# Moving bias and decoding work between engines in a fused attention and mixing kernel

## Chip, cores and metric

The kernel runs on one core of a Trainium2 chip. The metric is device time in microseconds, the median of several runs; lower is better. Engines: PE (TensorE: matmuls and transposes), DVE (VectorE), ACT (ScalarE), POOL (GpSimd), SP (issues the DMAs here). Each engine works through its own queue in order.

## What is computed

Two batches of 768 tokens, 8 heads of 64. Attention with a local window, a few global keys and a linear distance bias, then a two-layer channel mixer behind a layer norm, then a rotation by learned angles with token mixing.

```python
scores = q @ k.T / sqrt(64) + bias        # bias = -slope[h] * dist, heads h = 0..7
keep   = (key < n_global) | ((rel >= 0) & (rel < n_local))
attn   = softmax(where(keep, scores, -1e9)) @ v
x = attn + relu(layer_norm(attn) @ w_ch1) @ w_ch2
theta = x @ w_theta;  zr, zi = x * cos(theta), x * sin(theta)
u = x + w_tok_r @ zr + w_tok_i @ zi
out = u + relu(u @ w_ch)
```

The weights arrive as 64-bit floats ("pieces" of 128x512) and are turned into 32-bit floats on the chip.

## The kernel before

**Blocks and pairs.** The 12 blocks of 128 queries are worked in the order 0, 6, 1, 2, 3, 4, 5, 7, ... 11 (`SEQ`; a name such as e1_2_0 is batch 1, block 2 of that batch, head pair 0). Blocks 0 and 6 are first in their batches and see 128 keys, the others 256. Four head pairs make a block. `attention` is a pipeline over the 48 pairs: at step n it emits the scores of pair n (`scores`), the transposes of the probabilities of pair n-2 (`flip_probs`), and the values of pair n-3 (`values`). After a block come its copy from PSUM and scaling (`finish_x`: ACT writes xs, PE transposes it into xp, DVE scales), the layer norm, and a transposition for the mixer (`make_xt`: xnp on PE, xth on ACT, xtl on DVE).

**A pair** is: two score matmuls on PE; on DVE, per head, one operation that adds the bias and finds the maximum (L204, to nm and e); on ACT, per head, the exponential with its sum (L211); PE transposes e into pt; a copy of pt to pts on DVE for pairs 0 and 3 of a block (L226) and on ACT for pairs 1 and 2 (L224); PE multiplies with the values into xa.

**The bias** of each head is a table of 128 x 384. `make_bias` makes the part for first blocks on DVE before any score; the part for later blocks ("old", 128x256, eight heads) comes after the fourth head's maximum, on ACT (L148).

**Weight pieces.** `load_to` issues DMAs of raw pieces into three buffers. `decode` turns a raw piece into f32: for pieces 0 to 15 one activation (L314) and three DVE operations (L322 to L324); for later ones two activations (L314, L318) and two DVE operations (L319, L320). `split_w` then divides a piece into a high part (ACT, L340) and a low part (POOL or DVE, L341). Pieces 2f and 2f+1 belong to MLP group f. During attention, groups 0 to 3 (pieces 0 to 7) are used: for every chunk of two blocks, MLP steps `mlp_h` (12 matmuls, L369) and `mlp_o` (6 matmuls, L392). Pieces 8 to 15 wait in eight buffers for the next round.

**The order** of each engine's queue is set by the scheduler of the framework from the order of emission and priorities; `tc.issue_after(ins)` keeps an instruction behind another one (`behind_maximum(n)` uses it with the n-th maximum). `steps_to(n)` emits attention steps up to n, and the calls between them put the first decodings in the emission order.

Of the kernel before, what the change touches and what calls it, by code (L numbers as in the profile page):

```python
# [32 lines left out]
def kernel(ctx, tc, q, kwin, v, n_pair, g_ln, wall, out):  # L33
# [77 lines left out]
    nc.vector.memset(zero, 0.0)  # L111
    bias = [at.tile([P, WIN + P], BF16, name=f"bias{h}") for h in range(H)]

    maxima = []

    def behind_maximum(n):
        return tc.issue_after(maxima[n]) if n is not None else ExitStack()
# [1 line left out]
    def make_bias():  # L119

        n = WIN + P
        rel, key, a = (at.tile([P, n], F32, tag="xn", name=f"bias_{x}", bufs=3) for x in ("rel", "key", "a"))
        io = dict(allow_small_or_imprecise_dtypes=True)
        v_ = nc.vector
        own = rel[:, P:n].rearrange("p (t c) -> p t c", c=P)
        old, first = slice(0, WIN), slice(WIN, n)
        nc.gpsimd.iota(own, [[0, 2], [-1, P]], base=0, channel_multiplier=1, **io)
        nc.gpsimd.iota(key[:, first], [[1, P]], base=0, channel_multiplier=0, **io)
        nc.gpsimd.iota(rel[:, 0:PREV], [[-1, PREV]], base=PREV, channel_multiplier=1, **io)
        nc.gpsimd.iota(key[:, PREV:P], [[1, GLOB]], base=0, channel_multiplier=0, **io)  # L130
        v_.memset(rel[:, PREV:P], FAR)
        v_.memset(key[:, 0:PREV], FAR)
        v_.memset(key[:, P:WIN], FAR)
        v_.tensor_scalar(a[:, P:n], rel[:, P:n], 0.0, FAR, ALU.is_lt, ALU.mult)
        v_.tensor_tensor(rel[:, P:n], rel[:, P:n], a[:, P:n], ALU.max)
        yield
        load_n()
        for part in (first, old):
            r, k_, a_ = rel[:, part], key[:, part], a[:, part]
            with behind_maximum(3 if part is old else None):  # L140
                v_.tensor_scalar(a_, r, nl, NEG, ALU.is_ge, ALU.mult)
                v_.tensor_scalar(k_, k_, ng, NEG, ALU.is_ge, ALU.mult)
            v_.tensor_tensor(r, a_, r, ALU.subtract)
            v_.scalar_tensor_tensor(r, k_, nl, r, ALU.subtract, ALU.max)
            for h in range(H):
                slope = 2.0 ** (-8.0 * (h + 1) / H)
                if part is old:
                    nc.scalar.activation(bias[h][:, part], r, AF.Copy, scale=slope / SCALE)  # L148
                else:
                    v_.tensor_scalar(bias[h][:, part], r, slope / SCALE, None, ALU.mult)  # L150
            yield

    def slot(name):
# [30 lines left out]
    def scores(b, i, p, startup):  # L184
        nk = WIN if i else P
        b0 = 0 if i else WIN
        if p == 0:
            stat[b, i] = (
                at.tile([P, H], F32, tag="nm", name=f"nm{b}_{i}", bufs=2),
                at.tile([P, H], F32, tag="sm", name=f"sm{b}_{i}", bufs=2),  # L190
            )
        nm, sm = stat[b, i]
        qb, kb = qt[b, i], kt[b, i]
        s = [ps("h" if startup and p % 2 else "s", [P, nk], f"s{b}_{i}_{p}_{j}") for j in range(2)]
        k0 = WIN - nk
        for j in range(2):
            rows = slice(j * D, (j + 1) * D)
            nc.tensor.matmul(s[j], qb[rows, p, :], kb[rows, p, k0:WIN], start=True, stop=True)  # L198
        if startup:
            spin("o", f"spin{b}_{p}", 2)  # L200
        e = at.tile([P, 2, nk], F32, tag="p", name=f"e{b}_{i}_{p}", bufs=3)
        for j in range(2):
            h = 2 * p + j
            r = nc.vector.tensor_tensor_reduce(  # L204
                out=e[:, j, :], in0=s[j], in1=bias[h][:, b0:b0 + nk], scale=-SCALE, scalar=3.0e38,
                op0=ALU.add, op1=ALU.min, accum_out=nm[:, h:h + 1],
            )
            maxima.append(r.ins)
        for j in range(2):
            h = 2 * p + j  # L210
            nc.scalar.activation(e[:, j, :], e[:, j, :], AF.Exp, bias=nm[:, h:h + 1], scale=-1.0, accum_out=sm[:, h:h + 1])  # L211
        e_t[b, i, p] = e

    def flip_probs(b, i, p, startup):
# [5 lines left out]
            for c in range(nb):  # L220
                nc.tensor.transpose(pt[:, j, c, :], e[:, j, c * P:(c + 1) * P], ident)
        pts = at.tile([P, 2, nb, P], F32, tag="pt", name=f"pts{b}_{i}_{p}", bufs=2)
        if p % 3:
            nc.scalar.activation(pts, pt, AF.Copy)  # L224
        else:
            nc.vector.tensor_copy(pts, pt)  # L226
# [71 lines left out]
    def load_to(n):  # L298
        while n_staged[0] <= min(n, len(order) - 1):
# [3 lines left out]
            stage[i] = r  # L303
            n_staged[0] += 1

    def decode(i, out):

        n = n_decoded[0]
# [2 lines left out]
        assert order[n] == i  # L311
        r = stage.pop(i)
        load_to(n + NRAW)
        nc.scalar.activation(out, r.bitcast(F32)[:, :, 1], AF.Copy, scale=2.0**-112)  # L314
        t = rawp.tile([P, DM], I32, tag="dec", name=f"dec{i}", bufs=1)
        o = out.bitcast(I32)
        if i >= 4 * GROUP:
            nc.scalar.activation(t, r.bitcast(U32)[:, :, 0], AF.Copy, scale=2.0**-29 * (1 - 2.0**-15), bias=-0.4999)  # L318
            nc.vector.scalar_tensor_tensor(t, o, 3, t, ALU.logical_shift_left, ALU.bitwise_or)  # L319
            nc.vector.scalar_tensor_tensor(o, r[:, :, 1], -2**31, t, ALU.bitwise_and, ALU.bitwise_or)  # L320
# [277 lines left out]


    def general():  # L600
        es = ExitStack()
        ga = es.enter_context(tc.tile_pool(name="ga", bufs=1))
        row = ga.tile([P, S], F32, name="g_row")
# [175 lines left out]
    def steps_to(n):  # L779
        while n_step[0] < n:  # L780
            next(st, None)
            n_step[0] += 1
# [6 lines left out]
    next(bias_steps)  # L789
    load_to(1)  # L790
    nc.sync.dma_start(gbc, g_ln.partition_broadcast(P))
    steps_to(4)
    split_w(0)
    steps_to(done_at(0))
    split_w(1)
# [126 lines left out]
```

## Time and profile before

| | us |
|---|---|
| median of 3 runs | 571.13 (570.25 to 571.83) |
| profiled execution, its own time | 572.38 |
| its span | 570.5 |
| PE busy | 555.1 |
| DVE busy | 365.7 |
| ACT busy | 282.7 |
| POOL busy | 121.9 |

The span is what the profiler recorded between first and last instruction; the execution's own time lies a little over it. A busy time is the union of an engine's instructions. In lines of the timeline and of the chain, the first number is the start within the span, the second the duration.

### The profile page before, as it was taken

The numbers are of one execution on the slowest core, as the hardware profiler recorded it, in microseconds if no ns is written. First come the engines' busy times: TensorE is split into PE (matmuls) and PEld (weight loads), VectorE is DVE, ScalarE is ACT, GpSimd is POOL, SyncE is SP. The second block draws the span as 40 slices with busy tenths as digits, with TensorE's granted clock in tenths as the row PEclk, the third lists the DMA queues.
The fourth block names the chain that finished last, engine by engine and source line by source line (L and its number), as shares of the span: only waits on it lengthen the run. The fifth ranks groups of instructions, "written<-read, shape, count | busy, mean of one in ns | idle before, by whom it ended". The sixth has DMA issues, their size and how long they took to land.

```text
span 570.5 us, 9281 instructions
## 1 busy us (share of the span) xinstructions
PE 555.1 (97%) x3531; PEld 461.4 (81%) x3532; DVE 365.7 (64%) x789; ACT 282.7 (50%) x647; POOL 121.9 (21%) x103
## 2 busy tenths in 40 slices
PE   8898999999999999999999999999999999999996
PEld 4465676777888899999989888889888888888885
DVE  6899988857458732278784524462699879871442
ACT  5886864636226511166663415561578777740110
POOL 1455420000002100030300202231033347730000
PEclk9999999999999999999999999999999999999999
DMA  8965655500003410026552000000243200000112
GB/s 262 317 214 187 215 192 204 167 1 2 0 1 109 150 37 1 1 80 198 167 185 74 1 1 1 2 1 0 79 144 132 91 1 1 1 1 1 74 68 86
DMA packets 18548, 49.18 MB, mean 86 GB/s; under 512 B 2240, under 2 KB 4288, under 8 KB 18496
## 3 DMA queue, kind: packets, MB, share of 16 engines
q1 hardware_dynamic: 18496, 48.51, 25.7%
q8 instruction: 30, 0.49, 0.4%
q14 instruction: 22, 0.18, 0.1%
HBM read 45.35 MB, written 3.15 MB: 85 GB/s over the span
## 4 chain that ended last, share of the span: by engine, by line
PE 64%; ACT 1%; DVE 1%; issue 0%; DVEq 0%; ACTq 0%
PE acc L545 17%; PE op L392 17%; PE hp L369 17%; PE thm L480 6%; PE ch L591 6%; PE xp L284 1%; ACT wt L314 0%; ACT xth L285 0%; DVE hl L374 0%; DVE w2l L341 0%; DVE x2all L381 0%; ACT w L314 0%; ACT k L488 0%; ACT k L487 0%; ACT s L493 0%
## 5 line engine op out<-in xcount | busy, mean ns | idle before, releaser
L369 PE MATMUL hp<-xth,w1h 128*128 128x256 f32 x384 | 109.0, 284 | 0.0
L369 PE MATMUL hp<-xth,w1l 128*128 128x256 f32 x384 | 108.7, 283 | 0.0
L369 PE MATMUL hp<-xtl,w1h 128*128 128x256 f32 x384 | 108.4, 282 | 0.0
L374 DVE SCALAR_TENSOR_TENSOR hl<-hp,hh 128x256 fp32r<-128x256 f32 x96 | 40.3, 420 | 79.9 <-ACT hh L373 79.7
L373 ACT ACTIVATE hh<-hp 128x256 fp32r<-128x256 f32 x96 | 36.1, 377 | 95.5 <-PE hp L369 95.5
L545 PE MATMUL acc<-tokh,z 128*128 128x512 f32 (+1 forms) x320 | 79.6, 337 | 0.0
L392 PE MATMUL op<-w2h,hh 128*128 128x512 f32 x192 | 76.9, 401 | 0.7 <-ACT hh L373 0.5
L369 PEld LDWEIGHTS hp<-xth,w1h 128*128 128x128 f32 x384 | 72.6, 189 | 6.1 <-issue 1.5
L369 PEld LDWEIGHTS hp<-xtl,w1h 128*128 128x128 f32 x384 | 72.5, 189 | 5.9 <-issue 1.7
L392 PE MATMUL op<-w2h,hl 128*128 128x512 f32 x192 | 76.1, 396 | 0.0
L392 PE MATMUL op<-w2l,hh 128*128 128x512 f32 x192 | 76.1, 396 | 0.0
L369 PEld LDWEIGHTS hp<-xth,w1l 128*128 128x128 f32 x384 | 72.6, 189 | 1.7 <-issue 1.5
L545 PEld LDWEIGHTS acc<-tokh,z 128*128 128x128 f32 x320 | 55.3, 189 | 7.2
L211 ACT ACTIVATE e<-e,nm 128x256 f32<-128x256 f32 (+1 forms) x96 | 46.2, 482 | 25.3 <-DVE nm L204 23.8
L545 PE MATMUL acc<-tokl,z 128*128 128x512 f32 (+1 forms) x160 | 54.0, 338 | 0.0
L341 POOL TENSOR_TENSOR w1l<-w,w1h 128x512 fp32r<-128x512 f32 x16 | 22.3, 1393 | 136.9 <-ACT w1h L340 136.9
L381 DVE SCALAR_TENSOR_TENSOR x2all<-op,rsall,x2all 128x512 f32<-128x512 f32 x60 | 42.8, 743 | 6.8 <-PE op L392 6.8
L507 POOL TENSOR_TENSOR x2all<-xth,xtl 128x512 f32<-128x512 f32 x12 | 18.3, 1528 | 121.2 <-DVE k L499 116.2
L392 PEld LDWEIGHTS op<-w2h,hl 128*128 128x128 f32 x192 | 36.1, 188 | 9.2 <-DVE hl L374 0.4
L204 DVE CUSTOM_DVE_ANT_0 e<-s,bias 128x256 f32<-128x256 f32 (+1 forms) x96 | 35.5, 393 | 11.6 <-PE s L198 10.9
L457 DVE TENSOR_TENSOR tokl<-wt,tokh 128x512 fp32r<-128x512 f32 x36 | 33.9, 951 | 11.3 <-ACT tokh L456 11.1
L392 PEld LDWEIGHTS op<-w2h,hh 128*128 128x128 f32 x192 | 36.4, 190 | 5.6 <-ACT hh L373 0.7
(155 smaller groups left out, 1072.4 us busy)
## 6 DMA issues: line engine op xcount, KB each, us to landing
raw<-in_wall SPq DMA_DIRECT2D x58, 512.0 KB, 3.3
k<-in_kwin SPq DMA_DIRECT2D x10, 512.0 KB, 5.6
q<-in_q SPq DMA_DIRECT2D x12, 256.0 KB, 4.3
vc<-in_v SPq DMA_DIRECT2D x12, 256.0 KB, 3.3
out<-o SPq DMA_DIRECT2D x8, 256.0 KB, 2.0
vw<-in_v SPq DMA_DIRECT2D x10, 192.0 KB, 2.6
out<-o SPq DMA_DIRECT2D x8, 128.0 KB, 2.0
vw<-in_v SPq DMA_DIRECT2D x10, 64.0 KB, 3.5
```

Of the source, the lines that this page charges most:

```text
L204: r = nc.vector.tensor_tensor_reduce(out=e[:, j, :], in0=s[j], in1=bias[h][:, b0:b0 + nk], scale=-SCALE, scalar=3.0e38, op0=ALU.add, op1=A ...
L211: nc.scalar.activation(e[:, j, :], e[:, j, :], AF.Exp, bias=nm[:, h:h + 1], scale=-1.0, accum_out=sm[:, h:h + 1])
L341: (nc.vector if d and f >= GROUP else nc.gpsimd).tensor_tensor(lo, s, hi.bitcast(F32), ALU.subtract)
L369: nc.tensor.matmul(hp, l, r[:, kk, :], start=(n == 0), stop=(n == 3 * KD - 1))
L373: nc.scalar.activation(hh, hp, AF.Relu)
L374: nc.vector.scalar_tensor_tensor(hl, hp, 0.0, hh.bitcast(F32), ALU.max, ALU.subtract)
L381: nc.vector.scalar_tensor_tensor(x2[t], o, rsall[:, t:t + 1], x2[t], ALU.mult, ALU.add)
L392: nc.tensor.matmul(op_t[c][j], l, r, start=(f == fs[0] and n == 0), stop=(f == fs[-1] and n == 2))
L457: nc.vector.tensor_tensor(lo, src, hi.bitcast(F32), ALU.subtract)
L480: nc.tensor.matmul(mp, l[:, kk, :], r[:, kk, :], start=(n == 0), stop=(n == 3 * KD - 1))
L545: mm = nc.tensor.matmul(o, l[:, dsl], r[:, sl], start=first and not (paired and d % 2), stop=end and not (paired and d % 2 == 0))
L591: nc.tensor.matmul(mp, l[:, kk, es], r, start=(kk == 0 and m == 0), stop=(kk == KD - 1 and m == 2))
```

## The change

It moves work between engines and places in the order:

- The bias for later blocks is written by POOL (eight tensor_scalars of 128x256) instead of ACT.
- The first activations of pieces 0 and 1 are held behind the exponentials of pairs 5 and 6; `split_w(0)` is emitted after seven attention steps instead of four.
- Pieces 8 to 15 are decoded by two activations and two DVE operations instead of one and three, and the first activation of each is held behind the last exponential of a later block: the eighth block in `SEQ` for pieces 8 and 9, the ninth for 10 and 11, the tenth for 12 and 13, the eleventh for 14 and 15.
- From the seventh block in `SEQ` on, all four copies of pt to pts are by ACT.

```diff
-    maxima = []
+    maxima, exps = [], []
...
-                if part is old:
-                    nc.scalar.activation(bias[h][:, part], r, AF.Copy, scale=slope / SCALE)
-                else:
-                    v_.tensor_scalar(bias[h][:, part], r, slope / SCALE, None, ALU.mult)
+                (nc.gpsimd if part is old else v_).tensor_scalar(bias[h][:, part], r, slope / SCALE, None, ALU.mult)
...
-            nc.scalar.activation(e[:, j, :], e[:, j, :], AF.Exp, bias=nm[:, h:h + 1], scale=-1.0, accum_out=sm[:, h:h + 1])
+            r = nc.scalar.activation(e[:, j, :], e[:, j, :], AF.Exp, bias=nm[:, h:h + 1], scale=-1.0, accum_out=sm[:, h:h + 1])
+        exps.append(r.ins)
...
-        if p % 3:
+        if p % 3 or SEQ.index(b * NQ + i) >= 6:
             nc.scalar.activation(pts, pt, AF.Copy)
...
+    def behind_exponentials(i):
+
+        n = 5 + i if i < 2 else NPAIR * (7 + (i - 2 * GROUP) // 2) + 3 if 2 * GROUP <= i < 4 * GROUP else None
+        return tc.issue_after(exps[n]) if n is not None and n < len(exps) else ExitStack()
...
-        nc.scalar.activation(out, r.bitcast(F32)[:, :, 1], AF.Copy, scale=2.0**-112)
+        with behind_exponentials(i):
+            nc.scalar.activation(out, r.bitcast(F32)[:, :, 1], AF.Copy, scale=2.0**-112)
...
-        if i >= 4 * GROUP:
+        if i >= 2 * GROUP:
...
-    steps_to(4)
+    steps_to(7)
     split_w(0)
```

In the orders below the names carry batch, block and pair (w0 is piece 0, raw0 its raw form, dec0 the help buffer of its decoding), and each row is one instruction or several alike. The changed file has its lines 3 lower or 3 to 5 higher: L208 there is L211, L222 is L224, L318 and L322 are L314 and L318, L326 to L328 are L322 to L324.

ACT's queue at the start, before the change, from the second pair's exponentials on:

```order
L211 ACTIVATE e0_0_2_216,sm0_0_167<-e0_0_2_216,nm0_0_166 128x128
L148 ACTIVATE bias0_93<-bias_rel_111 128x256
...
L148 ACTIVATE bias7_100<-bias_rel_111 128x256
L211 ACTIVATE e0_0_2_216,sm0_0_167<-e0_0_2_216,nm0_0_166 128x128
L211 ACTIVATE e0_0_3_233,sm0_0_167<-e0_0_3_233,nm0_0_166 128x128 x2
L224 ACTIVATE pts0_0_1_241<-pt0_0_1_238 128x256
L314 ACTIVATE w0_246<-raw0_204 128x512
L314 ACTIVATE w1_256<-raw1_206 128x512
L211 ACTIVATE e1_0_0_290,sm1_0_282<-e1_0_0_290,nm1_0_281 128x128 x2
L224 ACTIVATE pts0_0_2_298<-pt0_0_2_295 128x256
```

Six more bias copies stand between the two shown; the decodings of pieces 0 and 1 are ahead of the fifth pair's exponentials (e1_0_0). With the change:

```order
L208 ACTIVATE e0_0_2_216,sm0_0_167<-e0_0_2_216,nm0_0_166 128x128
L222 ACTIVATE pts0_0_1_241<-pt0_0_1_238 128x256
L208 ACTIVATE e0_0_3_233,sm0_0_167<-e0_0_3_233,nm0_0_166 128x128 x2
L208 ACTIVATE e1_0_0_264,sm1_0_256<-e1_0_0_264,nm1_0_255 128x128 x2
L222 ACTIVATE pts0_0_2_272<-pt0_0_2_269 128x256
L208 ACTIVATE e1_0_1_283,sm1_0_256<-e1_0_1_283,nm1_0_255 128x128 x2
L208 ACTIVATE e1_0_2_302,sm1_0_256<-e1_0_2_302,nm1_0_255 128x128 x2
L248 ACTIVATE xs0_314<-xa0_0_243 128x512
L318 ACTIVATE w0_324<-raw0_204 128x512
L318 ACTIVATE w1_334<-raw1_206 128x512
L208 ACTIVATE e1_0_3_357,sm1_0_256<-e1_0_3_357,nm1_0_255 128x128 x2
```

The bias copies are gone from ACT, and both decodings stand seven rows later, behind the copy of block 0's result.

DVE's queue where the third block's maxima begin, with the change (before it, decoding 0 and decoding 1 stood ahead of the last pair of the second block, and the scaling of block 0 behind the first maximum here):

```order
L326 TENSOR_SCALAR dec0_330<-w0_324 128x512
L254 TENSOR_TENSOR x2all_66<-xp0_318,sm0_0_167 128x512
L327 SCALAR_TENSOR_TENSOR dec0_330<-w0_324,dec0_330 128x512
L266 BN_STATS bn0_370<-x2all_66 128x6
L328 SCALAR_TENSOR_TENSOR w0_324<-raw0_204,dec0_330 128x512
L267 BN_AGGR mv0_371<-bn0_370 128x2
L201 ISA e0_1_0_394,nm0_1_388<-s0_1_0_0_390,bias0_93 128x256
L201 ISA nm0_1_388 128x1
L326 TENSOR_SCALAR dec1_338<-w1_334 128x512
L274 TENSOR_SCALAR rsall_69<-mv0_371 128x1
L201 ISA e0_1_0_394,nm0_1_388<-s0_1_0_1_391,bias1_94 128x256
```

The first maximum of the third block (e0_1_0) is now behind all of decoding 0 and the statistics of block 0.

ACT's queue in a late run of attention (tenth to eleventh block), before:

```order
L211 ACTIVATE e1_3_3_1615,sm1_3_1433<-e1_3_3_1615,nm1_3_1432 128x256 x2
L224 ACTIVATE pts1_3_1_1625<-pt1_3_1_1620 128x512
L211 ACTIVATE e1_4_0_1646,sm1_4_1641<-e1_4_0_1646,nm1_4_1640 128x256 x2
L224 ACTIVATE pts1_3_2_1656<-pt1_3_2_1651 128x512
L211 ACTIVATE e1_4_1_1675,sm1_4_1641<-e1_4_1_1675,nm1_4_1640 128x256 x2
L211 ACTIVATE e1_4_2_1695,sm1_4_1641<-e1_4_2_1695,nm1_4_1640 128x256 x2
L250 ACTIVATE xs9_1711<-xa1_3_1627 128x512
```

and with the change:

```order
L208 ACTIVATE e1_3_3_1615,sm1_3_1433<-e1_3_3_1615,nm1_3_1432 128x256 x2
L222 ACTIVATE pts1_3_1_1625<-pt1_3_1_1620 128x512
L318 ACTIVATE w12_2266<-raw12_2152 128x512
L208 ACTIVATE e1_4_0_1646,sm1_4_1641<-e1_4_0_1646,nm1_4_1640 128x256 x2
L222 ACTIVATE pts1_3_2_1656<-pt1_3_2_1651 128x512
L318 ACTIVATE w13_2299<-raw13_2193 128x512
L208 ACTIVATE e1_4_1_1675,sm1_4_1641<-e1_4_1_1675,nm1_4_1640 128x256 x2
L222 ACTIVATE pts1_3_3_1685<-pt1_3_3_1680 128x512
L322 ACTIVATE dec13_2303<-raw13_2193 128x512
L208 ACTIVATE e1_4_2_1695,sm1_4_1641<-e1_4_2_1695,nm1_4_1640 128x256 x2
L222 ACTIVATE pts1_4_0_1705<-pt1_4_0_1700 128x512
L248 ACTIVATE xs9_1711<-xa1_3_1627 128x512
```

Two copies (pts1_3_3, pts1_4_0) and three decoding activations have come into these seven rows.

## Rows read from the trace of the kernel before

**Rows 1.** The page: busy time of the engines.

```profile
PE 555.1 (97%) x3531; PEld 461.4 (81%) x3532; DVE 365.7 (64%) x789; ACT 282.7 (50%) x647; POOL 121.9 (21%) x103
```

**Rows 2.** Stages: from:to, length, busy PE, PEld, DVE, ACT, POOL, clock, DMA, GB/s.

```profile
0.00:28.45 28.45, 24.69 (x137) 12.27 (x139) 21.04 (x100) 19.81 (x68) 7.41 (x16) 1.00 0.90 289
28.45:61.67 33.22, 30.40 (x246) 21.14 (x245) 31.00 (x92) 25.48 (x72) 17.59 (x14) 1.00 0.63 203
61.67:91.53 29.86, 28.57 (x217) 21.10 (x216) 27.98 (x80) 18.07 (x51) 9.34 (x8) 1.00 0.54 178
91.53:110.87 19.34, 18.64 (x151) 12.26 (x151) 15.84 (x54) 13.43 (x42) 0.55 (x1) 1.00 0.63 218
...
121.31:139.54 18.23, 17.39 (x149) 11.44 (x148) 11.76 (x46) 12.24 (x39) 0.55 (x1) 1.00 0.01 2
```

**Rows 3.** Waits of PE, 28 to 142 us: total, times, longest.

```profile
PE xnp L284 <- ACT xs L250: 3.5, 6, 1.2
```

**Rows 4.** Waits of ACT, 0 to 140 us: total, times, longest.

```profile
ACT w L314 <- DMA raw<-in_wall: 8.6, 7, 2.2
```

**Rows 5.** Timeline of the start, ACT and one maximum on DVE (idle before it).

```profile
9.65 2.56 ACT L148 ACTIVATE bias<-bias_rel 128x256 bf16<-128x256 f32 x8
...
11.82 0.29 DVE L204 CUSTOM_DVE_ANT_0 e<-s,bias 128x128 f32<-128x128 f32 x1 [0.54 <-PE s L198]
...
14.74 0.67 ACT L314 ACTIVATE w<-raw 128x512 f32<-128x512 f32 x1 [1.11 <-DMA raw<-in_wall]
...
16.60 0.39 ACT L211 ACTIVATE e<-e,nm 128x128 f32<-128x128 f32 x1
```

**Rows 6.** Timeline, PE and DVE: scores, xp, third block's first and last maximum.

```profile
8.34 0.49 PE L198 MATMUL s<-k,q 64*128 64x128 f32 x4
...
20.32 0.66 PE L255 MATMUL xp<-ident,xs 128*128 128x128 f32 x4 [0.15 <-ACT xs L250]
...
21.47 0.41 DVE L204 CUSTOM_DVE_ANT_0 e<-s,bias 128x256 f32<-128x256 f32 x1
...
28.02 0.42 DVE L204 CUSTOM_DVE_ANT_0 e<-s,bias 128x256 f32<-128x256 f32 x1
```

**Rows 7.** POOL's groups to 140 us: mean ns; idle before.

```profile
L272 POOL TENSOR_SCALAR xn<-x2all,mv 128x512 f32<-128x512 f32 x6 | 9.4, 1572 | 13.0 <-DVE mv L269 12.9
...
L127 POOL IOTA bias_rel<- 128x256 f32 x1 | 0.4, 356 | 0.0
```

**Rows 8.** DVE's groups, 61.67 to 91.53 us.

```profile
L324 DVE SCALAR_TENSOR_TENSOR w<-raw,dec 128x512 int32<-128x512 int32 x6 | 4.2, 697 | 0.0
...
L323 DVE SCALAR_TENSOR_TENSOR dec<-w,dec 128x512 int32<-128x512 int32 x6 | 4.1, 684 | 0.0
...
L322 DVE TENSOR_SCALAR dec<-w 128x512 int32<-128x512 int32 x6 | 3.0, 508 | 0.0
...
L226 DVE COPY pts<-pt 128x512 f32<-128x512 f32 x4 | 2.7, 686 | 0.1
```

**Rows 9.** Paces (timeline), the first split after attention, DMA issues of raw.

```profile
29.64 0.59 ACT L224 ACTIVATE pts<-pt 128x512 f32<-128x512 f32 x1
...
30.11 0.69 ACT L314 ACTIVATE w<-raw 128x512 f32<-128x512 f32 x1
...
169.95 0.63 ACT L340 ACTIVATE w1h<-w 128x512 fp32r<-128x512 f32 x1 [2.32 <-PE hp L369]
...
raw<-in_wall SPq DMA_DIRECT2D x58, 512.0 KB, 3.3
```

**Rows 10.** Waits of ACT in run A, then run B.

```profile
ACT e L211 <- DVE nm L204: 5.1, 4, 1.8
...
ACT e L211 <- DVE nm L204: 5.8, 7, 2.1
```

**Rows 11.** Timeline: DVE beside POOL.

```profile
18.72 1.26 POOL L341 TENSOR_TENSOR w1l<-w,w1h 128x512 fp32r<-128x512 f32 x1 [16.63 <-ACT w1h L340]
...
19.04 1.49 DVE L323 SCALAR_TENSOR_TENSOR dec<-w,dec 128x512 int32<-128x512 int32 x1
```

More of the change, by code (lines that the diff above doesn't have):

```diff
@@ L600, in general @@
     def general():
+        exps.clear()
         es = ExitStack()
```

## The prediction

> **What bounds the kernel now.** I read the page first: its own time 572.38 us lies about a span of 570.5 us in which TensorE is busy for 555.1 us [rows 1], and its chain of waits that ended last, long behind the attention, runs over TensorE's lines almost alone. Of the change hardly anything lies behind 141 us, so the second look is the table of stages [rows 2], cut where TensorE's work changes: start (to 28.45, where PE begins the first xnp), two stretches of attention mixed with first MLP steps, a run of attention (run A, 91.53 to 110.87), a pure MLP group, another run (run B, 121.31 to 139.54), the rest. The reader should see three things. The start keeps no engine full (ACT 19.81 of 28.45 us, PE partly on its spin matmuls) and the DMA engines at 0.90. From 28.45 to 91.53 DVE is the fullest after PE: 31.00 of 33.22 and 27.98 of 29.86 us. In runs A and B, PE is nearly full (idle 0.70 and 0.84 us) while ACT has slack: 13.43 of 19.34 and 12.24 of 18.23. From then on the end is PE's work alone: a microsecond won before 139.54 is a microsecond at the end, and at most 2.82 + 1.29 + 0.70 + 0.84 = 5.65 us of PE idleness lie between 28.45 and 139.54 to be won, besides the start. Third, who makes PE and ACT wait: PE mostly for ACT's copies of a block's result [rows 3], ACT for raw pieces not yet landed, 8.6 us in 7 waits [rows 4].
>
> **The change, part by part.**
>
> *Start.* ACT's eight bias copies hold its queue from 9.65 to 12.21 us; then it has two pairs' rest to do, stands 1.11 us before raw 0 until 14.74, takes raw 1 as well, and the exponentials of the fifth pair (block (1,0), pair 0) start at 16.60 [rows 5], though the second of their maxima began on DVE at 11.82. The change takes out the copies (2.56 us) and puts both decodings behind the result copy of block 0. So the fifth pair can run about 12.2. I follow PE from there with 0.4 to 0.5 us for each of its groups (a pair's scores, as in the row of 0.49, and its transposes, values and spins alike): values of block 0 end at 15.8 to 16.2, ACT's copy takes 0.6, and the four transposes of block 0's result (xp) start at 17.0 to 17.5; before the change they start at 20.32 [rows 6]. That is 2.8 to 3.3 us ahead. But DVE's queue now has most of decoding 0, the scaling of block 0 and its statistics in front of the third block's first maximum: 0.69 + 0.69 + 0.68 + 0.69 = 2.8 us behind a decoding that ACT can't begin before about 17.2. The first maximum of the third block then falls near 20.8 (before: 21.47) and its last, with decoding 1 in between, near 26.4 (before: 28.02) [rows 6]. The lead that reaches the first xnp transposes, which have the same PE work ahead of them in both orders, is thus about 1.5 us. Ends: 0, if raw 2, issued behind five loads of the fourth block now, lands late and holds ACT (its decoding stands between the two exponentials of the third block's first pair); 3.0, the lead at xp. **I take -1.5.**
>
> *Bias on POOL.* Eight tensor_scalars of 128x256. No row has one; nearest are POOL's tensor_scalar of 128x512, 1.57 us, and an iota of 128x256, 0.36 us [rows 7]. By half of the first, 0.79 each, they run from 9.6 to 15.9; at 0.36 to 12.5; at the full 1.57 to 22.2. POOL's next work came at 18.72 [rows 11], and its first xn follows only at about 21, and the third block needs the first bias pair at 20.8. Cost 0; if the cover is gone, see rival three.
>
> *Stretch 28.45 to 61.67.* Work is the same on every engine; DVE, 31.0 us, is the bound, with 2.2 us idle, part of it behind PE's wait for xs. In the new order PE puts MLP matmuls and the next block's first score ahead of the xnp transposes, where it waited (up to 1.2 us at once) [rows 3]. Ends: 0 (DVE still sets it, or raw 7, issued later, holds ACT) and -1.2. **I take -0.5.**
>
> *Stretch 61.67 to 91.53.* DVE loses here three operations each for six pieces, 3.0 + 4.1 + 4.2 = 11.3 us, and three of the four copies at 0.69 [rows 8]: 13 of its 28 us. ACT gets three copies and one activation instead of six decodings, which had their part in its 8.6 us of waiting for pieces. What is left is PE: its 1.29 us idle can go. Ends 0 and -1.29; **-0.9**, since PE's xnp must still await a copy by ACT.
>
> *Runs A and B.* DVE loses 4 copies in each, and pieces come in with two DVE operations instead of three, so it has air. ACT gets the copies and, of the sixteen activations of pieces 8 to 15, most: eight in each run (two such stood in run A before). In a full queue instructions overlap by 0.1 us: a copy of 0.59 takes 0.47 (29.64 to 30.11), a decoding activation of 0.69 thus 0.58 [rows 9]. Run A: 13.43 + 4 x 0.47 + 6 x 0.58 = 18.8 of 19.34 us. Run B: 12.24 + 4 x 0.47 + 8 x 0.58 = 18.8, more than its 18.23. ACT comes level with PE. Its waits for maxima there, 5.1 and 5.8 us [rows 10], must take up nearly all of it. Run A: PE's 0.70 us (it waited for a copy behind a landing piece) is won or lost again, **0**, ends -0.7 and +1.0. Run B: **+0.5**, ends -0.3 and +2.
>
> *Queues.* On SP raws 2, 7 and 11 to 15 fall behind the fourth to twelfth block's loads. Raw 12 now waits behind k of the last block, whose buffer comes free with the scores of block (1,2); ACT wants it three pairs (over 5 us) later, and a raw lands in 3.3 us in the median [rows 9]. Cost 0 while that holds. The hold is on a piece's first activation only; the second (dec) of pieces 8 and 12 goes ahead of it, on data long landed or due: 0. All pieces up to 15 are decoded by the end of run B; the first of them was split at 169.95 [rows 9], so later decoding costs nothing behind it.
>
> Sum: -1.5 - 0.5 - 0.9 + 0 + 0.5 = **-2.4 us**. The profiled execution (572.38) is 1.25 us over the median of the runs, 571.13; the difference is carried to the median: **568.7 us**. A measurement of this kernel can tell about 0.3%, 1.7 us, from no change: faster means under 569.4, slower over 572.8.
>
> **Rivals.**
> 1. *The lead is given back to ACT in its queue* (570.0 to 572.0, at 570.9). The 2.9 us of the first three terms are real, but runs A and B lose 0.7 and 2 us, as ACT's added work fits into only part of its waits. For: 18.8 us in 18.23. Against: no decoding there waits for DMA any more, and the order puts each where PE has MLP matmuls between.
> 2. *ACT becomes the bound of both runs* (slower). Same place, but half of the 5.1 and 5.8 us in which ACT waits for maxima can't be filled, because every decoding stands in order ahead of exponentials that PE needs. The runs grow by 2.6 and 2.9 us, 5.5 in all; less the 2.9 of the other terms, +2.6: 573.7. It decides as soon as about 4.6 of the 10.9 us can't be used (2.9 + 1.7). Against: transposes lag scores by two pairs, and eight pairs take 18.23 us in run B, so ACT has some 2 x 2.3 us to catch up.
> 3. *POOL's bias slows DVE's start.* Beside POOL's two-input subtraction at 18.72, DVE's two-input operation took 1.49 us [rows 11], against 0.69 undisturbed [rows 8]. If POOL is at 1.57 a piece it still runs to 22.2, beside the four two-input operations of decodings 0 and 1: 4 x 0.8 = 3.2 us, the startup term becomes +1.7 and the time 571.9. The Trainium skill says the like (GPSIMD Engine Reference, Specifications): POOL shares its SBUF interfaces with VectorE and contends with DVE instructions that have two SBUF inputs or run in a two-port mode. By that rule the trace agrees with the 1.49. The same page (Engine selection) holds one-input POOL work to be roughly at line rate, an estimate of 0.2 us for 256 columns, by which the eight would be over near 11.5 and this rival void; the 1.57 us for 512 columns here speaks against it.
>
> That the change does not do what it says can be left out: the order shows each move.
>
> **Chances.** Forecast 0.52 (566.2 to 569.4); rival 1 0.24; rival 3 0.10; rival 2 0.14. So faster 0.52, same 0.34, slower 0.14. The range reaches from 566.2 (start at its better end, or both middle stretches at theirs) through rivals 1 and 3 to 572.6; left out are most of rival 2 and a little below.
>
> **What would show it.** Right: in the new profile the first xnp near 27 us, no ACT activity between 9.6 and 12.2 but exponentials, ACT's waits for raw far under 8.6 us; the MLP group after run A starting near 108 instead of 110.87; run B at 18 to 19.5 us with ACT busy over 17 of it. Wrong: a first xnp at 28 or later (then the start gave nothing; look at raw 2 before w2 on ACT, or at stretched DVE operations beside L147), or run B over 20 us with PE waiting for ACT's pts (rival 2), or new ACT waits for raw 11 to 15.

## The result, and the profile after

The changed kernel takes 577.45 us (median of 6 runs, 576.32 to 579.54), the kernel before 571.48 in the same comparison: a ratio of 1.0105, 95% interval 1.0075 to 1.0135. It is slower by about 6 us; 568.7 was forecast, and 577.45 lies above the range. The profiled execution took 576.76 us, 4.4 more than that of before, about a span of 574.6 (before: 570.5). The page's first part, to be set beside [rows 1]:

```profile
PE 562.2 (98%) x3531; PEld 464.5 (81%) x3532; DVE 356.2 (62%) x769; ACT 290.0 (50%) x659; POOL 129.2 (22%) x111
```

ACT has 7 us more to do and DVE 10 less, as the change means it; but TensorE, with the same 3531 matmuls, is busy for 7.1 us more.

The stages are cut anew, each where TensorE has issued the same matmuls of every kind in both kernels; a run of attention and the pure MLP group behind it go together. Stages of before that [rows 2] doesn't hold (from:to, length, busy PE, PEld, DVE, ACT, POOL, granted clock, DMA share, GB/s):

```profile
91.53:121.31 29.78, 29.08 (x217) 21.43 (x216) 23.07 (x68) 15.40 (x46) 1.10 (x2) 1.00 0.46 159
121.31:150.55 29.24, 28.40 (x217) 21.07 (x216) 18.75 (x60) 14.34 (x44) 1.10 (x2) 1.00 0.01 2
150.55:570.50 419.95, 413.99 (x2503) 364.36 (x2502) 243.89 (x392) 189.57 (x367) 85.36 (x61) 1.00 0.17 57
```

The same six stages of the changed kernel, to be set against these and the first three of [rows 2]:

```profile
0.00:29.53 29.53, 26.49 (x138) 13.05 (x139) 21.04 (x99) 18.35 (x62) 14.66 (x24) 0.93 0.88 289
29.53:63.18 33.65, 32.10 (x245) 22.23 (x245) 30.20 (x90) 24.47 (x68) 16.45 (x14) 0.96 0.53 176
63.18:93.99 30.81, 30.50 (x218) 21.98 (x217) 18.91 (x62) 17.05 (x49) 9.37 (x9) 1.00 0.38 122
93.99:123.73 29.74, 29.11 (x217) 21.54 (x216) 21.62 (x64) 20.19 (x56) 1.10 (x2) 1.00 0.50 160
123.73:153.51 29.78, 29.16 (x218) 21.58 (x217) 21.71 (x64) 20.33 (x56) 1.09 (x2) 1.00 0.22 72
153.51:574.60 421.09, 414.83 (x2503) 364.13 (x2502) 242.72 (x391) 189.64 (x368) 86.53 (x61) 1.00 0.17 57
```

Three readings. First, the differences are +1.08, +0.43, +0.95, -0.04, +0.54 and +1.14 us, 4.1 in all: nearly every stage is longer. Second, TensorE's granted clock is not 1.00 in the first two. Third, TensorE idles less: over the first five stages, length less busy time is 6.2 us where it was 9.4, so the waits did go, and its busy time grew by more. Who made whom wait, 0 to 154 us (total, times, longest):

```profile
PE pt L219 <- ACT e L208: 1.4, 1, 1.4
...
PE xnp L282 <- ACT xs L248: 0.5, 1, 0.5
```

```profile
ACT w L318 <- DMA raw<-in_wall: 1.4, 1, 1.4
```

PE's wait for xs fell from 3.5 to 0.5 us [rows 3], ACT's for raw from 8.6 to 1.4 [rows 4], as the prediction said. Two things took back more than that.

**The clock.** Timeline of TensorE in the changed kernel (start, duration, what; idle before it):

```profile
16.69 0.66 PE L253 MATMUL xp<-ident,xs 128*128 128x128 f32 x4
...
21.58 0.70 PE L195 MATMUL s<-k,q 64*128 64x256 f32 x2
23.71 0.33 PE L219 MATMUL pt<-ident,e 128*128 128x128 f32 x1 [1.43 <-ACT e L208]
...
27.34 1.11 PE L219 MATMUL pt<-ident,e 128*128 128x128 f32 x4
28.38 1.22 PE L195 MATMUL s<-k,q 64*128 64x256 f32 x2
29.53 1.11 PE L282 MATMUL xnp<-ident,xn 128*128 128x128 f32 x4
```

The transposes of the first result (xp) start 3.6 us earlier than before [rows 6]. At 22.28 TensorE runs dry for 1.43 us: the exponential that it needs stands on ACT behind the decoding of raw 2, which began only at 22.50. Soon after, its operations take nearly twice as long (xnp 1.11 for the 0.66 of before). The stages say why:

```profile
23.00:25.40 2.40, 1.69 (x6) 0.86 (x6) 1.92 (x6) 2.28 (x9) 2.40 (x3) 1.00 0.76 283
25.40:32.20 6.80, 6.80 (x27) 4.16 (x26) 4.00 (x15) 4.73 (x13) 1.31 (x2) 0.50 0.73 244
32.20:36.00 3.80, 3.80 (x40) 2.55 (x36) 3.80 (x14) 2.97 (x10) 2.05 (x2) 1.00 0.01 3
```

From 25.4 to 32.2 us the granted clock is 1.2 GHz, not 2.4. TensorE is busy for all of it, so by an estimate from the two levels 6.8 us do the work of 3.4. The whole execution has a mean granted clock of 0.994; in the other five it is 0.989 to 0.992. That mean also counts the last microseconds, in which TensorE has finished and a lower clock costs nothing (the 0.998 of before comes from its last 2.7 us alone, behind the last matmul at 565.5), so it doesn't tell how much more the other five lost here.

**Lone heads.** A pair's two score matmuls read partitions 0 to 63 and 64 to 127. In before's timeline one pair at 26.60, and a head that has other work on both sides at 27.82, read:

```profile
26.60 0.70 PE L198 MATMUL s<-k,q 64*128 64x256 f32 x4
27.24 0.65 PE L221 MATMUL pt<-ident,e 128*128 128x128 f32 x4
27.82 0.70 PE L198 MATMUL s<-k,q 64*128 64x256 f32 x2
28.45 0.66 PE L284 MATMUL xnp<-ident,xn 128*128 128x128 f32 x4
```

(Each head leaves two records.) Two heads side by side take 0.70, one alone takes 0.70 as well: neighbours run at the same time. That half-arrays work in parallel is also what the Trainium skill says (TensorEngine Tiling (Array Packing), Key Properties); the trace agrees. From the start to the next operation of another kind is 0.64 us for the pair (0.63 for others) and 0.63 for the lone head, so each lone one costs 0.31 us more. In the changed kernel, around the eighth block's first pair:

```profile
73.99 0.70 PE L195 MATMUL s<-k,q 64*128 64x256 f32 x2 [0.20 <-DVE nm L201]
74.62 0.66 PE L282 MATMUL xnp<-ident,xn 128*128 128x128 f32 x4
75.11 0.60 PE L253 MATMUL xp<-ident,xs 128*128 128x128 f32 x4
75.64 0.70 PE L195 MATMUL s<-k,q 64*128 64x256 f32 x2
```

This is the "next block's first score ahead of the xnp transposes" that the prediction counted as cover for PE's wait. Only one head stands there; its partner comes behind xp. The scores have two PSUM banks: the first head waited for DVE's maximum on one of them, and the maximum on the other ran from 73.85 to 74.27. That the scheduler parts the pair for this reason is likely, but no run shows it. The order of the changed kernel has 16 lone heads of 256 keys, that of before 4: two more in the first stage, two in the second, four in the third, two in each run. Twelve more at 0.31 are 3.8 us, more than the 3.3 us of waiting that went.

### The profile page after: what moved, and what is told of

It reads as the page before. It is cut to its first block, busy times and chain, and to the rows that moved or that the text cites. A ratio compares the mean times of both kernels' runs of the same rounds, so it can differ in the third digit from the quotient of the medians.

```text
span 574.6 us, 9278 instructions
## 1 busy us (share of the span) xinstructions
PE 562.2 (98%) x3531; PEld 464.5 (81%) x3532; DVE 356.2 (62%) x769; ACT 290.0 (50%) x659; POOL 129.2 (22%) x111
## 3 DMA queue, kind: packets, MB, share of 16 engines
q1 hardware_dynamic: 18496, 48.51, 25.2%
## 4 chain that ended last, share of the span: by engine, by line
PE 47%; DVE 3%; ACT 2%; DMA 1%; issue 1%; DVEq 0%; SPq 0%; ACTq 0%
PE acc L549 17%; PE op L396 9%; PE hp L373 8%; PE thm L484 6%; PE ch L595 6%; DMA raw<-in_wall 1%; DVE dec L323 1%; ACT dec L322 1%; PE xp L282 1%; DVE w L324 1%; DVE thr L324 0%; ACT wt L318 0%; DVE hl L378 0%; DVE w2l L345 0%; ACT xth L283 0%
## 5 line engine op out<-in xcount | busy, mean ns | idle before, releaser
L208 ACT ACTIVATE e<-e,nm 128x256 f32<-128x256 f32 (+1 forms) x96 | 46.1, 482 | 21.0 <-DVE nm L201 20.7
L201 DVE CUSTOM_DVE_ANT_0 e<-s,bias 128x256 f32<-128x256 f32 (+1 forms) x96 | 35.4, 393 | 20.7 <-PE s L195 19.7
L511 POOL TENSOR_TENSOR x2all<-xth,xtl 128x512 f32<-128x512 f32 x12 | 19.5, 1624 | 119.7 <-DVE k L503 119.7
L322 ACT ACTIVATE dec<-raw 128x512 int32<-128x512 uint32 x50 | 33.4, 668 | 19.0 <-DVE wt L324 8.0
```

The lines of the kernel that those rows point to most:

```text
L201: r = nc.vector.tensor_tensor_reduce(out=e[:, j, :], in0=s[j], in1=bias[h][:, b0:b0 + nk], scale=-SCALE, scalar=3.0e38, op0=ALU.add, op1=A ...
L208: r = nc.scalar.activation(e[:, j, :], e[:, j, :], AF.Exp, bias=nm[:, h:h + 1], scale=-1.0, accum_out=sm[:, h:h + 1])
```

## Experiments

Times are medians; a ratio is to the runs of before in the same comparison. The kernel before has executions with a lower clock too: of its 105 runs in these comparisons 32 had a mean clock under 0.995. Its runs with 0.996 or more have medians of 571.5 to 572.1 in the four comparisons, so medians of kernels whose clock stays up can be set beside each other to about half a microsecond. Stage lengths come from one profile each. The third to fifth stage agree to 0.03 us among three kernels with the change's order of heads, and among three with heads together. Before's order differs more between profiles (second stage 33.22 and 32.52, third 29.86 and 30.41, fourth 29.78 and 28.85), and over all kernels the last stage differs by 1.8 us.

### The start alone

Without the later hold, the two ACT operations for pieces 8 to 15 and the added copies by ACT:

```diff
-        if p % 3 or SEQ.index(b * NQ + i) >= 6:
+        if p % 3:
...
-        n = 5 + i if i < 2 else NPAIR * (7 + (i - 2 * GROUP) // 2) + 3 if 2 * GROUP <= i < 4 * GROUP else None
+        n = 5 + i if i < 2 else None
...
-        if i >= 2 * GROUP:
+        if i >= 4 * GROUP:
```

> The first two parts of the change alone: bias of later blocks on POOL, first decodings behind pairs 5 and 6. Theory 1 (raw 2 is issued too late; ACT waits for it, TensorE waits for ACT at about 22 to 24 us, and its granted clock falls to 1.2 GHz for 6.8 us behind that, which costs 3.4 us; and score matmuls whose other head stands elsewhere in the order cost 0.31 us each, 6 more of them than before): 573.5 to 576, with the clock at 0.5 from about 25 to 32 us in the profile. Theory 2 (the loss comes from the later part, ACT's added copies and decodings): 569 to 570.5, and the clock at 1.0 throughout.

574.96 us, ratio 1.0049 (1.0009 to 1.0088). The clock was 1.2 GHz from 25.2 to 35.4 us, and in all 7 runs the mean clock was 0.991 or less. The start part brings the lower clock with it.

### The later part alone

The start of before under the change's other edits:

```diff
-                (nc.gpsimd if part is old else v_).tensor_scalar(bias[h][:, part], r, slope / SCALE, None, ALU.mult)
+                if part is old:
+                    nc.scalar.activation(bias[h][:, part], r, AF.Copy, scale=slope / SCALE)
+                else:
+                    v_.tensor_scalar(bias[h][:, part], r, slope / SCALE, None, ALU.mult)
...
-        n = 5 + i if i < 2 else NPAIR * (7 + (i - 2 * GROUP) // 2) + 3 if 2 * GROUP <= i < 4 * GROUP else None
+        n = NPAIR * (7 + (i - 2 * GROUP) // 2) + 3 if 2 * GROUP <= i < 4 * GROUP else None
...
-    steps_to(7)
+    steps_to(4)
```

> The other two parts alone: pieces 8 to 15 behind later blocks and by two ACT operations, all copies of probabilities by ACT from the seventh block on. Theory 1: no fall of the clock; about 1 us of TensorE's idle time goes, and 6 more lone score matmuls cost 1.9 us: 571.5 to 573.5. Theory 2 (ACT's added work is the cause): 574.5 to 577.

573.92 us, ratio 1.0043 (1.0000 to 1.0087). The clock in the profile stayed at 2.4 GHz, but 5 of the 12 runs had a mean clock under 0.99 and took 578.5 to 580.7; the six with 0.996 or more have a median of 572.8, against 571.9 for such runs of before. The profile was 0.9 us ahead of before at the cut behind run A's MLP group (0.7 of it already at 61 us, where the later part begins), 0.3 at the next, 0.7 behind at the end. The new lone heads of runs A and B are there (130 us, as at 73.99 above). Not the 3 to 5 us that a bound by ACT would give.

### Raw 2 early

```diff
     nc.sync.dma_start(gbc, g_ln.partition_broadcast(P))
+    load_to(2)
     steps_to(7)
```

> The whole change, with the DMA of raw 2 issued ahead of the fourth block's loads as in the kernel before; TensorE's order is otherwise that of the change. Theory 1: ACT's wait of 1.4 us for raw 2 and TensorE's of 1.4 us behind it go, the clock stays at 2.4 GHz, 3.5 to 5 us are won: 572 to 574. Rival (POOL's bias slows DVE's start, or the later part is the cause): 576.5 to 578.

576.96 us, ratio 1.0084 (1.0062 to 1.0106): half a microsecond less, which the intervals don't tell from nothing, where 3.5 to 5 were expected. ACT no longer waits for raw. Who made PE wait, 12 to 30 us, and the stages:

```profile
PE s L195 <- DVE nm L201: 1.0, 2, 0.8
```

```profile
23.00:25.40 2.40, 1.61 (x8) 0.79 (x6) 2.40 (x7) 1.33 (x4) 2.40 (x2) 1.00 0.77 296
25.40:32.20 6.80, 6.80 (x29) 3.99 (x27) 5.16 (x17) 5.52 (x16) 2.13 (x3) 0.63 0.87 274
32.20:36.00 3.80, 3.80 (x30) 2.80 (x30) 3.06 (x12) 1.98 (x8) 2.48 (x3) 0.76 0.03 10
```

My theory was wrong in this point: raw 2 is not the root. With it on time TensorE waits for DVE, which is busy for all of 23.00 to 25.40 with the decoding of piece 1 among the third block's maxima. The wait of 0.8 stands behind this operation, twice as long as its like in piece 0 (0.67):

```profile
23.23 1.41 DVE L328 SCALAR_TENSOR_TENSOR w<-raw,dec 128x512 int32<-128x512 int32 x1
```

There is a hole anyway, and the clock falls behind it.

### Spin matmuls in the hole

```diff
         for j in range(2):
+            if (b, i, p, j) == (0, 1, 0, 1):
+                spin("o", "fill", 8)
             for c in range(nb):
                 nc.tensor.transpose(pt[:, j, c, :], e[:, j, c * P:(c + 1) * P], ident)
```

> The whole change, with eight more spin matmuls (bf16, result unused) on TensorE among the scores and transposes of the stretch in which it waited at 22 to 24 us; raw 2 stays late. Theory 1 with the idle time as what brings the clock down: ACT still waits for raw 2, but the clock stays at 2.4 GHz and some 3 us are won: 573.5 to 575. Rival (the wait itself is the cost and the clock falls whatever TensorE does there): 577 to 579, with the clock at 0.5 behind 25 us as before.

573.64 us, ratio 1.0031 (1.0007 to 1.0055), 3.8 us less than the change by the medians. ACT still waits 1.3 us for raw 2, and the clock stays up:

```profile
23.00:25.40 2.40, 2.40 (x12) 1.06 (x12) 1.89 (x6) 2.40 (x9) 2.40 (x3) 1.00 0.63 225
25.40:32.20 6.80, 6.63 (x50) 4.27 (x49) 6.38 (x24) 6.05 (x19) 2.06 (x3) 1.00 0.75 252
```

The scheduler spread the eight over the queue from 20.2 us on, among scores and transposes. The mean clock was 0.998 or more in 11 of 12 runs. Eight matmuls whose result nobody reads make the changed kernel faster.

### Nine more pairs apart, in the kernel before

The price of a lone head by itself. The transposes of the pair two steps back go between the two heads, for pairs 1 and 2 of the last four blocks (`between` flips that pair and returns its last transpose). A ninth pair came apart in the scheduler's order with these eight:

```diff
         for j in range(2):
             rows = slice(j * D, (j + 1) * D)
-            nc.tensor.matmul(s[j], qb[rows, p, :], kb[rows, p, k0:WIN], start=True, stop=True)
+            r = between() if j and between else None
+            with tc.issue_after(r) if r is not None else ExitStack():
+                nc.tensor.matmul(s[j], qb[rows, p, :], kb[rows, p, k0:WIN], start=True, stop=True)
```

> The kernel before, with nine more pairs of blocks 8 to 11 of the batch order whose two score matmuls stand apart in TensorE's order, other work between them (18 more lone matmuls of 256 keys); no operation is added. Theory 1 (two neighbouring heads share the array and take 0.63 us together, a lone one takes 0.63 by itself, 0.31 us more each): 18 x 0.31 = 5.6 us longer than before, ratio 1.008 to 1.011. Rival (the place of a head costs nothing, since other matmuls run meanwhile): ratio 1.000 to 1.003.

577.33 us, ratio 1.0064 (1.0027 to 1.0100); the span grew by 4.5 us, the two stages with the split pairs by 2.1 and 2.0:

```profile
91.42:123.32 31.90, 31.75 (x218) 22.61 (x217) 23.58 (x68) 15.72 (x46) 1.10 (x2) 1.00 0.45 149
123.32:154.57 31.25, 30.75 (x217) 22.18 (x217) 19.23 (x60) 14.68 (x44) 1.10 (x2) 1.00 0.01 2
```

TensorE's score matmuls in these two stages took, in the kernel before and here (line, operation, count | busy us, mean ns | idle):

```profile
L198 PE MATMUL s<-k,q 64*128 64x256 f32 x64 | 11.6, 428 | 0.0
```

```profile
L200 PE MATMUL s<-k,q 64*128 64x256 f32 x64 | 17.5, 428 | 0.0
```

The same 64 records of the same 428 ns cover 5.9 us more: 0.33 for each of the 18 lone heads. Some 0.9 us of it fell into waits that TensorE had there anyway, so 0.23 each shows at the end of the two stages. The price is real; in the time it comes out a little under my 0.31, and the ratio under the 1.008 to 1.011 that I expected.

### Heads held together

The change, with the heads of one pair kept side by side where it parts them (`last_xp`, `last_xa` hold the last transpose of xp and the last value matmul emitted):

```diff
+        n = SEQ.index(b * NQ + i) * NPAIR + p
+        hold = last_xp[0] if p == 0 and n >= 20 else last_xa[0] if n == 26 else None
+        with tc.issue_after(hold) if hold is not None else ExitStack():
             for j in range(2):
                 rows = slice(j * D, (j + 1) * D)
                 nc.tensor.matmul(s[j], qb[rows, p, :], kb[rows, p, k0:WIN], start=True, stop=True)
```

> The whole change, with both heads of the first pair of the sixth to twelfth block held behind the last transpose of xp, and those of one more pair behind the values ahead of them: 8 lone score matmuls of 256 keys fewer than in the change; raw 2 late and the clock as there. Theory 1: 2.5 us less by the matmuls, 0.5 to 1 us of waiting for xs back: 1.5 to 2 us faster than the change, 575 to 576, ratio to before about 1.007. Rival (TensorE's waits come back in full and nothing is won): 577 to 578.

575.93 us, ratio 1.0024 (0.9988 to 1.0060): 1.5 us less than the change. The third, fourth and fifth stage, each with two lone heads fewer, took 30.25, 29.20 and 29.23 us: 0.56, 0.54 and 0.55 less than in the change. The other profiles repeat it: 30.80 to 30.82, 29.74 to 29.77 and 29.76 to 29.78 in the three kernels with the change's order of heads, 30.23 to 30.26, 29.20 to 29.23 and 29.23 in the three with these heads together. The clock was at 1.2 GHz from 23.4 to 33.7 us, and under 0.995 in all 12 runs.

### Both remedies

The two edits above in one kernel, with the rest of the change as it is; the eight spins are emitted ahead of both heads' transposes here:

```diff
+        hold = last_xp[0] if p == 0 and n >= 20 else last_xa[0] if n == 26 else None
+        with tc.issue_after(hold) if hold is not None else ExitStack():
...
+        if (b, i, p) == (0, 1, 0):
+            spin("o", "fill", 8)
```

> The change with the eight spin matmuls and with the heads held together: both causes of theory 1 taken out. Theory 1: 1.5 to 2 us less than the change with spins alone (573.6), 571.5 to 572.5; level with before or up to 1 us faster than it. Rival (the change is slow for a third reason, such as ACT's added work): 573 to 575, ratio to before 1.003 or more.

571.07 us, ratio 0.9961 (0.9930 to 0.9993), 6.4 us less than the change and the first version ahead of before: by 1.0 us against the 20 of 35 runs of before whose mean clock was 0.996 or more (median 572.05). Its first five stages:

```profile
0.00:27.98 27.98, 26.49 (x144) 12.97 (x147) 20.83 (x99) 17.32 (x59) 14.70 (x24) 1.00 0.90 290
27.98:60.07 32.09, 30.59 (x245) 21.28 (x244) 30.03 (x90) 25.13 (x72) 16.76 (x14) 1.00 0.61 202
60.07:90.33 30.26, 29.68 (x218) 21.60 (x217) 18.91 (x63) 16.86 (x49) 8.86 (x9) 1.00 0.36 119
90.33:119.56 29.23, 28.45 (x217) 21.22 (x216) 21.44 (x64) 20.10 (x56) 1.54 (x2) 1.00 0.50 162
119.56:148.79 29.23, 28.46 (x217) 21.22 (x216) 21.50 (x64) 20.10 (x56) 1.54 (x2) 1.00 0.22 73
```

Taking out the two causes together takes out the whole loss.

### The later part with heads together

The start of before, the change's later part, and a hold on the first pair of the eighth, tenth and twelfth block.

```diff
+        hold = last_xp[0] if n in (28, 36, 44) else None
```

> The later part of the change alone, with the heads of the first pair of the eighth, tenth and twelfth block together: 6 lone matmuls fewer than in the later part alone, none more than before. Theory 1: 1 to 2 us less than the later part alone (its profile ended 0.7 us behind that of before): 0.3 to 1.3 us faster than before, ratio 0.998 to 0.9995. Rival (TensorE waits for xs in place of it): no change against the later part alone, ratio 1.001 to 1.004.

571.94 us, ratio 1.0004 (0.9959 to 1.0048). The median is 2.0 us under that of the later part alone, but the interval is wide: inconclusive as a verdict on before. In 3 of its 12 runs, and in 5 of 12 of the later part alone, the mean clock was under 0.99; the runs with 0.996 or more have medians of 571.45 (7 runs) and 572.80 (6). Its third to fifth stage took 29.47, 29.22 and 29.22 us, those of the later part alone 29.76, 29.75 and 29.76.

### Spin matmuls in before's own hole

```diff
         vc, vw = vt[b, i]
+        if (b, i, p) == (0, 0, 3):
+            spin("o", "fill", 4)
```

> The kernel before with four more spin matmuls in the stretch at 16.4 to 17.8 us in which TensorE waits for a copy by ACT (one pair's heads come apart there, 0.6 us, next to that wait). In the runs so far the kernel before had a mean clock under 0.99 in 8 of 35 executions, and those were 5 to 8 us longer. If holes of TensorE in the start are what brings the clock down, at most 1 of about 10 runs falls under 0.99, and the median is 571 to 572.5. Rival (the falls have nothing to do with that hole): about a quarter of the runs still under 0.99, median 572 to 574.

572.32 us, ratio 0.9995 (0.9972 to 1.0018). None of 12 runs had a mean clock under 0.997; of the 29 runs of the kernel before in the same comparison 5 were under 0.99, at 577.9 to 579.9 us. With the kernel below, which has the same spins, no run in 24 fell. So the kernel before lives near the same edge, and there too the spins take the fall away; no profile of that start shows where it falls. They don't make it faster otherwise: the 19 runs of before with a mean clock of 0.996 or more have a median of 571.94.

### The later part on that start

The kernel with the later part and heads together, plus the same four spin matmuls:

```diff
+        if (b, i, p) == (0, 0, 3):
+            spin("o", "fill", 4)
```

> The later part of the change with the heads together, on the start of before with the same four spin matmuls. Against the spin matmuls alone it tells what the later part is worth: theory 1, 0.5 to 1 us faster (570.5 to 571.5), by TensorE's idle time up to 140 us less about 0.5 us behind it; rival (the later part is worth nothing once heads are together): the same as with spin matmuls alone.

572.10 us, ratio 0.9992 (0.9972 to 1.0011), against 572.32 with the spins alone: the rival holds. The later part is worth 0.2 us by the medians, less than the runs of either kernel differ by (1.1 and 2.0 us).

### Both remedies and raw 2 early

```diff
     nc.sync.dma_start(gbc, g_ln.partition_broadcast(P))
+    load_to(2)
     steps_to(7)
```

> The whole change with spin matmuls and heads together, and raw 2 issued early besides. With the clock held, ACT's wait of 1.3 us for raw 2 may be all that is left of it. If that wait is on the path: the first xnp 0.5 us earlier than with raw 2 late (27.98), 570.3 to 571. Rival (DVE's decoding of piece 1, in front of the third block's maxima, sets it anyway): the same as without, 570.8 to 571.5.

571.05 us, ratio 0.9966 (0.9941 to 0.9992); the first xnp at 28.24 with xp at 17.06 (27.98 and 16.81 with raw 2 late). The rival holds: nothing won.

### The start with both remedies, without the later part

The kernel of the first experiment with the eight spins, and one pair held:

```diff
+                spin("o", "fill", 8)
...
+        hold = last_xa[0] if n == 34 else None
```

> The start part of the change alone, with the eight spin matmuls and one pair held together: as many lone score matmuls as in the whole change with both remedies (571.1), without the later part. If the later part costs in TensorE's queue behind 150 us what it wins before (its profile: 0.9 us ahead at 121 us, 0.7 behind at the end): within 0.7 us of the whole change with both remedies, 570.4 to 571.8. If the later part is worth the 0.9 us: 571.7 to 572.5; if it costs on balance: under 570.4.

571.02 us, ratio 0.9980 (0.9963 to 0.9996): the same median as with the later part (571.07), in another comparison. Against the 10 of 17 runs of before with a mean clock of 0.996 or more (571.46) 0.4 us is won. What is won over before comes with the start part, as far as these runs can tell.

## Why the prediction was wrong

By its own steps. Of the measured differences, the clock's share is an estimate (half of 4.1 us at 1.2 GHz before the first xnp, half of 2.7 behind it). The last column is the same difference for the changed kernel with eight spins in the hole, whose clock stayed up:

| term | forecast | measured | of it clock | rest | with spins |
|---|---|---|---|---|---|
| start | -1.5 | +1.08 | 2.06 | -0.98 | -0.53 |
| 28.45 to 61.67 | -0.5 | +0.43 | 1.35 | -0.92 | -0.42 |
| 61.67 to 91.53 | -0.9 | +0.95 | 0 | +0.95 | +0.94 |
| run A and MLP group | 0 | -0.04 | 0 | -0.04 | -0.02 |
| run B and MLP group | +0.5 | +0.54 | 0 | +0.54 | +0.52 |
| behind | 0 | +1.14 | 0 | +1.14 | +0.36 |

- **Start.** The mechanism was right: xp 3.6 us ahead (forecast 2.8 to 3.3), then DVE in front. The step that failed is the one that is missing: after "I follow PE from there" nothing asks where PE, now early, would run dry, nor what its clock does behind that. I read 1.00 in every stage [rows 2] as a constant of the kernel; 6.8 us at 1.2 GHz came in its place, about 3.4 us. The end that I named for this term (raw 2 holds ACT) did come, yet raw 2 early changed nothing, because DVE's decoding was level with it. The lead was mis-sized as well: with the clock up (and the spins in the queue) 0.53 us of it reach the first xnp, not 1.5. There the third block's last maximum starts at 27.16, for the 26.4 of the forecast. The sign that I gave for a failing start, a first xnp at 28 or later, came with 29.53; of the two causes named beside it, the wait for raw 2 costs nothing by itself, and stretched DVE operations are the next point.
- **Bias on POOL.** Cost 0, as forecast; its eight operations, 0.86 us each, were over at 16.80, before decoding 0 began on DVE at 17.14, whose two-input operations ran at 0.68. Decoding 1 was stretched, beside other work of POOL, the layer norm's xn and the split of piece 0:

```profile
9.89 6.91 POOL L147 TENSOR_SCALAR bias<-bias_rel 128x256 bf16<-128x256 f32 x8 [7.80 <-DVE bias_rel L144]
...
21.81 1.45 POOL L271 TENSOR_TENSOR xn<-xn,gbc 128x512 f32<-128x512 f32 x1
23.23 1.72 POOL L345 TENSOR_TENSOR w1l<-w,w1h 128x512 fp32r<-128x512 f32 x1
```

```profile
21.45 0.68 DVE L327 SCALAR_TENSOR_TENSOR dec<-w,dec 128x512 int32<-128x512 int32 x1
...
22.39 1.42 DVE L328 SCALAR_TENSOR_TENSOR w<-raw,dec 128x512 int32<-128x512 int32 x1
```

  So what rival 3 feared came from POOL work that it didn't name: 0.7 us in this operation, and 0.4 in the first of decoding 1 (0.83 us at 20.29, beside POOL's scaling for xn, where that of decoding 0 took 0.43). Both stand ahead of maxima of the third block and may be what the lead lost. Before, the one operation of [rows 11] was stretched like this. No run takes POOL's work away from there.

- **Stretches 28.45 to 91.53.** The step that failed is "in the new order PE puts MLP matmuls and the next block's first score ahead of the xnp transposes": I booked a gain and no price. In the third stage PE's idle time fell from 1.29 to 0.31 us as forecast, and two pairs apart cost 1.25 by the price of 0.31 a head. On before's start, with no head apart there, the later part took 29.47 us for this stage instead of 29.86: without the price, 0.4 of the 0.9 that I booked came. What remains of the stage in the change, about 0.7 us, I saw only as single switches between kinds of matmul that take 0.1 to 0.2 longer; no run took them apart. The second stage's -0.9 is not firm either: with the clock held it was -0.42, and where the split pairs were put into before, the first 91 us are the same program, and that profile took 32.52 us for this stage instead of 33.22 (and 30.41 for the third instead of 29.86).
- **Runs A and B.** ACT, 20.2 us busy in 29.7, did not become the bound; the sums of 0 and +0.5 came out, but for another reason than mine: the heads of a pair apart cost in run A as much as PE's waits gave back, and in run B more. With heads together both take 29.23. Before's length of run A is not firm: the same order behind before's start with spins took 28.85, without the one wait of 0.7 us for a copy by ACT.
- **Behind.** before took 419.9 us there. The nine profiles with the later part took 419.7 to 421.3, the four others without it 419.6 to 420.6: the +1.14 is within what profiles differ by. Whether some of it belongs to the later part stays open.
- **The rivals.** Rival 2 had the right sign for the wrong reason; rival 3's bias was over before the decodings, though DVE was stretched by other work as above. None held a price for the order of TensorE's own queue. "Slower" had 0.14. Two readings were off, without weight in the outcome: from 28.45 to 61.67 DVE (31.00) was fuller than PE (30.40), not the fullest after it; and the range's end of 566.2 needs the start and both middle stretches at their better ends together, not one or the other.

## What to carry to other kernels

Before crediting a filler that the scheduler moves into a wait, look at what it is torn from: matmuls on half the partitions are only half price beside their partner, and a diff of the order shows each pair that comes apart. When a change makes TensorE arrive early, look for the place where it then runs dry; if its clock falls there, the price is a multiple of the wait (here about 3.4 us more behind a wait of 1.43), and a few matmuls without purpose are cheaper. Two remedies that each undo one cause, and then both together, tell more than undoing parts of the diff: by parts, each half of this change looked guilty.

## What was not expected of the hardware

- In the start of the changed kernel, and of the three variants with that start and no spins, the mean clock was under 0.995 in all 31 runs; with eight spins there, in 1 of 48. The hole that precedes the fall (TensorE busy 3.30 of the 5 us from 20 to 25 in the change) is not deeper than the one that before has at 15 to 20 us (2.91 of 5), whose clock stays up in most executions (73 of 105 with a mean of 0.995 or more). First before, then the change:

```profile
15.00:20.00 5.00, 2.91 (x21) 1.29 (x18) 3.79 (x8) 4.39 (x17) 1.26 (x1) 1.00 1.05 362
```

```profile
20.00:25.00 5.00, 3.30 (x15) 1.51 (x12) 4.68 (x15) 3.62 (x11) 4.76 (x4) 1.00 0.90 340
25.00:30.00 5.00, 5.00 (x18) 2.70 (x19) 2.79 (x13) 3.49 (x12) 1.71 (x2) 0.54 0.76 240
```

- Why the one hole always costs the clock and the other seldom does, these runs don't settle.
